# Last feature pair of two token groups: from tile products to seven block products

## The chip, the cores and the metric

The kernel runs on one core of a Trainium2 chip. The time is the device time of one launch, in microseconds. The engines are named as in the profile: PE (TensorE, the matrix products), PEld (its weight loads), DVE (VectorE), ACT (ScalarE), POOL (GpSimd) and SP (SyncE, whose queue issues the transfers). PE writes its products into PSUM, of which a core has eight banks here, each 128 x 512 fp32. POOL works on SBUF alone.

## The reference, cut to what matters

Retention over 4 x 8 heads gives 3072 tokens of 512 features. Two feed-forward layers follow:

```
h = x @ w_in;   g = h * sigmoid(1.702 h);        x = g @ w_out          (d_ff 2048)
gate = sigmoid(x @ w_gate);  val = x @ w_val;    out = (gate*val) @ w_out   (d_ff 1536)
```

All is fp32. The change lies in the second layer, the last part of the kernel.

## The kernel before, in words

**Splits.** A product of fp32 matrices is made of three matmuls on operands split in two, high part times high, high times low, low times high. A split of a tile is two instructions: ACT casts the tile to its high part (h), and another engine subtracts that from the tile to get the low part (l).

**The second layer.** The tokens go in NG = 3 groups g of 1024, the 1536 features in QS = 6 pairs q of 256. For each group and pair there are two chains n, one for the gate (m = 0) and one for the value (m = 1), 36 chains in all. A chain multiplies the group's x by a 512 x 256 slice of the weights as a 2 x 2 block product with seven block products instead of eight (Winograd's form). `product` (L652) is one of them: six matmuls of 128 x 512. The seven are named by their operands: A11 B11 in `begin` (L728); A12 B21, S2 T2, S1 T1 and S3 T3 in `middle` (L737); A22 T4 and S4 B22 in `finish` (L768). A11 B11, S2 T2, S3 T3 and A22 T4 add up in one PSUM bank `a`; S1 T1 and S4 B22 in another, `d`. Between the additions ACT copies bank `a` out, once after each of A11 B11 (m1), S2 T2 (u2) and S3 T3 (u3), and `c22` (L763) is added by DVE from bank `d` and u3. `consume` (L700) takes each of the four results: for a gate chain the sigmoid, for a value chain the product of gate and value (DVE, L712) and its split (ACT L721, DVE L723).

**The group's x operands.** T1 = B12 - B11, T2 = B22 - T1, T3 = B12 - B22 and T4 = B21 - T2 are made from x by POOL, and B11, B21, T1, T2, T3, T4 and B22 are split in two halves k. The tiles of the splits exist once, so an operand of the next group can only be split once the last chain of the present one has used it. `prep_late` (L546) is a generator that makes them for groups 1 and 2: first the loads from `x2d`, then the differences, then the splits. The border loop calls it step by step.

**The output product.** The features of a pair times 256 rows of w_out are again a block product with seven parts, `out_seven` (L845), for the pairs q = 0 to 4: seven steps, each of two times six matmuls of 128 x 256 (L853), and after each step DVE adds the two banks to `part` in SBUF (L868; once per pair, by an ACT copy L865 and a POOL addition L866 instead). It needs four sums of the feature blocks, S1 to S4, made by POOL in `g_sums` (L680) and split in `g_parts` (L691), one at each call of `pump` (L667), and eight products of w_out blocks, made ahead by `out_job` (L793) during the last units of the first layer and kept in DRAM as `wtd`. `load_wt` (L839) brings them in, one copy at a time. For pair q = 5 no such sums are made: `out_pair` (L903) multiplies the eight 128-token tiles of the group by both features directly, six matmuls of 128 x 512 for each tile (L911), and `evict` (L918) adds the bank to `part` on DVE and stores the tile's rows.

**The order around the border of two groups** is written out by hand in the loop from L1171: each engine runs its instructions in the order in which the loop emits them. For the pair q = 5, with chains n and n + 1: `middle(n)`, the seven steps of pair 4 around `finish(n)`, `begin(n+1)`, `load_wt(5)`, the loads of the next chain's weights, `middle(n+1)`, two half tile products, `finish(n+1)`, the rest of the tile products with an eviction and a step of `prep_late` behind each, and `begin(n+2)`. The borders are those behind chains 11 and 23; the third group has none.

## Time and profile before

| | us |
|---|---|
| median of 3 runs (1145.3 to 1145.57) | 1145.51 |
| the profiled execution | 1146.02 |
| its span, first to last instruction | 1144.3 |
| PE busy | 1138.4 |
| DVE busy | 803.3 |
| ACT busy | 584.8 |
| POOL busy | 582.9 |

The span is what the engines' instructions cover; the profiled execution's time holds 1.7 us more around it. Busy times are sums over instructions; PE's instructions overlap in the pipeline, so its busy time is not work at its peak rate. An instruction's row gives its start, its time, its line in the kernel and, in brackets, how long its engine had idled before it and what ended that. A row of several instructions gives their sum. The chain that ended last is followed backwards from the end: it shows which engine's work the time consists of.

### The profile page before, as it was taken

How to read it: one execution, taken by the hardware profiler on the slowest of the kernel's cores; microseconds unless marked ns; L12 is line 12 of the kernel's file. 1: busy time of each engine (PE TensorE's matmuls, PEld its weight loads, DVE VectorE, ACT ScalarE, POOL GpSimd, SP SyncE). 2: the span in 40 equal slices, each digit the busy share in tenths (PEclk: the TensorE clock that was granted, in tenths of full speed). 3: DMA queues.
4: the chain of work that ended last, by engine and by line, in shares of the span. 5: the costliest groups of instructions: out<-in, count | busy, mean ns of one | idle time of the engine just before them, and what ended most of it. 6: DMA issues, size and time to landing. Idle time of an engine off the chain costs nothing.

```text
span 1144.3 us, 17967 instructions
## 1 busy us (share of the span) xinstructions
PE 1138.4 (99%) x6610; PEld 964.2 (84%) x6610; DVE 803.3 (70%) x1085; ACT 584.8 (51%) x1048; POOL 582.9 (51%) x439
## 2 busy tenths in 40 slices
PE   9999999999999999999999999999999999999998
PEld 8778888888888888888888888888888888888887
DVE  6988768777777667775663788776566676566666
ACT  4676665566565556655554544445433334543331
POOL 5578765555645445554454687776222256222220
PEclk9999999999999999999999999999999999999999
DMA  9855745565454544523205476678655556655533
GB/s 343 270 162 180 228 127 186 173 212 194 150 192 147 166 146 160 194 82 120 83 19 191 173 281 226 224 262 309 224 191 193 193 203 247 249 193 194 193 129 111
DMA packets 83139, 215.09 MB, mean 188 GB/s; under 512 B 9194, under 2 KB 13802, under 8 KB 83052
## 3 DMA queue, kind: packets, MB, share of 16 engines
q1 hardware_dynamic: 82608, 213.55, 54.7%
q8 instruction: 52, 0.85, 0.3%
q10 hardware_dynamic: 444, 0.40, 0.1%
q14 instruction: 35, 0.29, 0.1%
HBM read 155.46 MB, written 58.46 MB: 187 GB/s over the span
## 4 chain that ended last, share of the span: by engine, by line
PE 92%; DVE 3%; POOL 2%; issue 1%; DMA 1%; ACT 1%; SPq 0%; DVEq 0%; POOLq 0%; ACTq 0%
PE pa L658 16%; PE pd L658 8%; PE po L853 8%; PE acc L435 7%; PE h L325 7%; PE h L327 7%; PE h L326 7%; PE acc L437 7%; PE acc L436 7%; PE pb L658 4%; PE pa L853 2%; PE pd L853 2%; PE h L133 2%; PE po L911 2%; PE h L191 1%
## 5 line engine op out<-in xcount | busy, mean ns | idle before, releaser
L310 POOL TENSOR_TENSOR wl<-wraw,wh 128x512 fp32r<-128x512 f32 x110 | 156.6, 1431 | 176.6 <-ACT wh L309 167.0
L683 POOL TENSOR_TENSOR raw<-raw,raw 128x512 f32<-128x512 f32 x60 | 89.9, 1519 | 180.0 <-DVE raw L712 178.8
L325 PE MATMUL h<-xh,wh 128*128 128x512 f32 x380 | 149.0, 392 | 0.0
L435 PE MATMUL acc<-gh,wh 128*128 128x512 f32 x376 | 148.4, 395 | 0.2 <-DVE half L450 0.2
L327 PE MATMUL h<-xh,wl 128*128 128x512 f32 x380 | 148.1, 390 | 0.2 <-POOL wl L310 0.2
L326 PE MATMUL h<-xl,wh 128*128 128x512 f32 x380 | 147.9, 389 | 0.0
L437 PE MATMUL acc<-gl,wh 128*128 128x512 f32 x376 | 146.5, 390 | 0.0
L436 PE MATMUL acc<-gh,wl 128*128 128x512 f32 x376 | 146.3, 389 | 0.0
L344 DVE TENSOR_TENSOR gl<-sg,gh 128x512 fp32r<-128x512 f32 x94 | 102.5, 1091 | 52.8 <-ACT gh L343 51.6
L336 DVE TENSOR_TENSOR sg<-h,sg 128x512 f32<-128x512 f32 x94 | 64.8, 689 | 85.8 <-ACT sg L335 85.7
L309 ACT CAST wh<-wraw 128x512 fp32r<-128x512 f32 x190 | 110.8, 616 | 14.5 <-PE acc L437 11.0
L335 ACT ACTIVATE sg<-h 128x512 f32<-128x512 f32 x94 | 56.2, 598 | 113.9 <-PE h L327 111.2
L658 PE MATMUL pa<-xoh,oh 128*128 128x512 f32 x288 | 112.5, 391 | 0.0
L658 PE MATMUL pa<-xol,oh 128*128 128x512 f32 x288 | 112.4, 390 | 0.0
L658 PE MATMUL pa<-xoh,ol 128*128 128x512 f32 x288 | 112.1, 389 | 0.0
L343 ACT CAST gh<-sg 128x512 fp32r<-128x512 f32 x94 | 58.2, 621 | 74.8 <-DVE sg L336 74.7
L327 PEld LDWEIGHTS h<-xh,wl 128*128 128x128 f32 x380 | 71.3, 188 | 16.1 <-POOL wl L310 1.2
L435 PEld LDWEIGHTS acc<-gh,wh 128*128 128x128 f32 x376 | 70.6, 188 | 16.8 <-ACT wh L309 0.6
L325 PEld LDWEIGHTS h<-xh,wh 128*128 128x128 f32 x380 | 71.3, 188 | 15.3 <-issue 0.5
L326 PEld LDWEIGHTS h<-xl,wh 128*128 128x128 f32 x380 | 71.3, 188 | 15.2 <-issue 0.5
L437 PEld LDWEIGHTS acc<-gl,wh 128*128 128x128 f32 x376 | 70.6, 188 | 15.1
L436 PEld LDWEIGHTS acc<-gh,wl 128*128 128x128 f32 x376 | 70.6, 188 | 14.2
(217 smaller groups left out, 2835.4 us busy)
## 6 DMA issues: line engine op xcount, KB each, us to landing
w<-in_w_dram SPq DMA_DIRECT2D x68, 512.0 KB, 4.1
in_t<-in_qkv_dram SPq DMA_DIRECT2D x95, 256.0 KB, 4.4
oh<-wcd SPq DMA_DIRECT2D x24, 512.0 KB, 3.8
ol<-wcd SPq DMA_DIRECT2D x24, 512.0 KB, 4.8
w2d<-cva SPq DMA_DIRECT2D x36, 256.0 KB, 2.2
oh<-wcd SPq DMA_DIRECT2D x24, 384.0 KB, 3.2
ol<-wcd SPq DMA_DIRECT2D x24, 384.0 KB, 4.0
raw<-w2d SPq DMA_DIRECT2D x26, 256.0 KB, 3.5
```

What stands on the lines that cost most here:

```text
L309: nc.scalar.copy(wh, raw)
L310: lo_engine.tensor_tensor(out=wl, in0=raw, in1=wh, op=ALU.subtract)
L325: nc.tensor.matmul(bank[:, :n], wh[:, k, :], xh[:, k, :n], start=(k == 0), stop=False)
L326: nc.tensor.matmul(bank[:, :n], wh[:, k, :], xl[:, k, :n], start=False, stop=False)
L327: nc.tensor.matmul(bank[:, :n], wl[:, k, :], xh[:, k, :n], start=False, stop=(k == KC - 1))
L344: nc.vector.tensor_tensor(out=gl[:, :n], in0=sg[:, :n], in1=gh[:, :n], op=ALU.subtract)
L435: nc.tensor.matmul(a, wh[:, wc], gh[:, :n], start=st, stop=False)
L436: nc.tensor.matmul(a, wl[:, wc], gh[:, :n], start=False, stop=False)
L437: nc.tensor.matmul(a, wh[:, wc], gl[:, :n], start=False, stop=sp)
L658: nc.tensor.matmul(bank, w[:, kk], x[:, k, :], start=start and k == 0 and w is wh and x is xh, stop=stop and k == 1 and w is wl, skip_grou ...
L683: nc.gpsimd.tensor_tensor(out=out_, in0=in0, in1=in1, op=op)
L853: nc.tensor.matmul(bank[:, t * 256:(t + 1) * 256], a[:, sl], b[:, w, :], start=start and not t and a is gh and b is wh, stop=a is gl, skip ...
```

## The change

For q = 5 of groups 0 and 1 the tile products are replaced by `out_seven` with its seven steps, its `part` sums and now its stores (`store`), with bank `b` used again in place of a new `d`. Therefore `consume` makes the sums S1 to S4 there too, `out_job(5)` prepares all eight blocks (two groups of units more, `OUT_AT`), and `load_wt` brings seven of them. The steps are laid around the first chain of the next group: step 1 behind `finish(n+1)`, step 2 behind `begin(n+2)`, and steps 3 to 7 inside `middle(n+2)`, between S2 T2 and S1 T1 (`ahead2`). `prep_late` splits each operand in one step, half k = 0 on DVE and half k = 1 on POOL; its loads for k = 1 go into the free `raw8` tile. B11 and B21 are split inside `middle(n+1)` ahead of S1 T1, T2 behind it, and T1, T3, T4 and B22 between steps 3 to 7. The third group keeps the tile products, which read their four blocks from other places of `wtd`.

```diff
         0: (34, 35, 38, 39, 40, 42), 1: (41, 42, 43, 46, 47, 48), 2: (51, 52, 54, 55, 56, 58),
-        3: (66, 67, 68, 70, 71, 72), 4: (72, 73, 74, 75, 76, 78), 5: (82, 83, 84),
+        3: (66, 67, 68, 70, 71, 72), 4: (72, 73, 74, 75, 76, 78), 5: (82, 83, 84, 85, 86, 87),
     }
...
     NC0 = 2 * QS
-    OT1, OT2, OT3, OT4, OB21, OB22, OB11 = range(7)
+    OT1, OT2, OT3, OT4, OB21, OB22, OB11, OB12 = range(8)
     wcd = [dram.tile([P, 14, 256], F32, name=f"wcd{n}") for n in range(NC0)]
-    wtd = [[dram.tile([P, 7, 256], F32, name=f"wtd{q}{x}") for x in "hl"] for q in range(QS)]
+    wtd = [[dram.tile([P, 8 if q == QS - 1 else 7, 256], F32, name=f"wtd{q}{x}") for x in "hl"] for q in range(QS)]
     p2 = {}
...
         p2["w"].append(pool(ctx, "wo", 1, "left"))
-        p2["xu"] = pool(ctx, "xu", 3, "left")
+        p2["xu"] = pool(ctx, "xu", 2, "left")
         for name, bufs in (("part", 1), ("tmp", 1), ("g7", 1), ("wt", 1), ("raw7", 5), ("ct", 2)):
...
+        t = p2["w"][0].tile([P, 8, 256], F32, name="raw8", tag="raw8")
         for k in range(2):
-            for j, half, kk in ((B11, 0, k), (B12, 1, k), (B22, 1, k + 2), (B21, 0, k + 2)):
-                raws[k][j] = tile1("raw7" if k and j == B21 else "xu" if k else "xt")
+            for e, (j, half, kk) in enumerate(((B11, 0, k), (B12, 1, k), (B22, 1, k + 2), (B21, 0, k + 2))):
+                raws[k][j] = t[:, 2 * e:2 * e + 2, :].rearrange("p a c -> p (a c)") if k else tile1("xt")
                 nc.sync.dma_start(out=raws[k][j], in_=x2d[2 * g + half][:, kk, :])
...
-        def split(k, j, engine):
-            h, l = hl[j]
-            nc.scalar.copy(h[:, k, :], raws[k][j])
-            engine.tensor_tensor(out=l[:, k, :], in0=raws[k][j], in1=h[:, k, :], op=ALU.subtract)
+        def split(j, engine=nc.gpsimd):
+            for k in range(2):
+                h, l = hl[j]
+                nc.scalar.copy(h[:, k, :], raws[k][j])
+                (engine if k else nc.vector).tensor_tensor(
+                    out=l[:, k, :], in0=raws[k][j], in1=h[:, k, :], op=ALU.subtract
+                )
...
             for j in (T1, T2):
-                raw[j] = p2["ct"].tile([P, 512], F32, name="ct", tag="ct") if k else tile1("xt")
+                raw[j] = tile1("xu" if k else "xt")
             diff(k, T1, B12, B11)
...
             yield
-        for j in (B11, B21):
-            for k in range(2):
-                split(k, j, nc.gpsimd)
-            yield
-            yield
-        for k in range(2):
-            split(k, T2, nc.gpsimd if k else nc.vector)
+        split(B11)
+        yield
+        split(B21)
+        yield
+        split(T2)
         for k in range(2):
...
         for j in (T1, T3, T4, B22):
-            for k in range(2):
-                split(k, j, nc.gpsimd if k else nc.vector)
-                yield
+            split(j)
+            yield
...
         yield
-        if j == A21 and q < QS - 1:
+        if j == A21 and chains[n] != (NG - 1, QS - 1, 1):
             g_sums()
...
-    def middle(n):
+    def middle(n, ahead2=lambda: None, behind2=lambda: None):
...
         pump()
+        ahead2()
         product(n, d, S1, T1, True, True)
...
         pump()
+        behind2()
         cb[n] = [a, d, u2, c22]
-    def finish(n, last):
+    def finish(n, last, border=False):
         a, d, u2, c22 = cb.pop(n)
...
         add(d, d, u2)
-        pump()
+        if not border:
+            pump()
         next(x12)
...
         next(x12)
-        if last:
+        if last or border:
             next(x12)
...
             t = p2["w"][0].tile([P, 8, 256], F32, name="raw8", tag="raw8")
-            w0, w1_ = t[:, :2], t[:, 2:4]
+            w0, w1_, sa, sb = (t[:, 2 * j:2 * j + 2] for j in range(4))
         else:
...
+        yield
         if plain:
-            h = p2["w"][0].tile([P, 4, 256], F32R, name="oh0", tag="oh0")[:, :2]
-            todo = [(w0, slice(0, 2), slice(0, 2)), (w1_, slice(0, 2), slice(2, 4))]
+            t = p2["w"][0].tile([P, 4, 256], F32R, name="oh0", tag="oh0")
+            hs = [t[:, :2], t[:, 2:4]]
         else:
-            yield
             sa = in_p.tile([P, 2, 256], F32, name="half", tag="half", bufs=3)
             sb, h = (g_p.tile([P, 2, 256], x, name="ost", tag="ost") for x in (F32, F32R))
-            op(sa[:, 0], w0[:, 1], w0[:, 0])
-            op(sa[:, 1], w1_[:, 1], sa[:, 0])
-            yield
-            todo = [
-                (w0, slice(0, 1), slice(OB11, OB11 + 1)),
-                (w1_, slice(0, 2), slice(OB21, OB22 + 1)),
-                (sa, slice(0, 2), slice(OT1, OT2 + 1)),
-                (sb, slice(0, 2), slice(OT3, OT4 + 1)),
-            ]
+            hs = [h, h]
+        op(sa[:, 0], w0[:, 1], w0[:, 0])
+        op(sa[:, 1], w1_[:, 1], sa[:, 0])
+        yield
+        n = 2 if plain else 1
+        todo = [
+            (w0, slice(0, n), slice(OB11, OB11 + n)),
+            (w1_, slice(0, 2), slice(OB21, OB22 + 1)),
+            (sa, slice(0, 2), slice(OT1, OT2 + 1)),
+            (sb, slice(0, 2), slice(OT3, OT4 + 1)),
+        ]
         for j, (t, sl, to) in enumerate(todo):
+            h = hs[j % 2]
             nc.scalar.copy(h[:, sl], t[:, sl])
...
             l = t.bitcast(F32R)
-            if not plain and not j:
+            if not j:
                 op(sb[:, 0], w0[:, 1], w1_[:, 1])
...
-    def load_wt(q):
+    def load_wt(q, plain=False):
         wt[:] = [p2["wt"].tile([P, 7, 256], F32R, name=f"wt{x}", tag=f"wt{x}") for x in "hl"]
-        n = 4 if q == QS - 1 else 7
+        pieces = [(0, OB11, 2), (2, OB21, 2)] if plain else [(0, 0, 7)]
         for x in range(2):
-            nc.sync.dma_start(out=wt[x].bitcast(F32)[:, :n, :], in_=wtd[q][x][:, :n, :])
-
-    def out_seven(q):
+            for to, a, n in pieces:
+                nc.sync.dma_start(out=wt[x].bitcast(F32)[:, to:to + n, :], in_=wtd[q][x][:, a:a + n, :])
+
+    def out_seven(q, g=None):
...
+        def store(s, half, e):
+            if g is not None:
+                r0 = g * 1024 + half * 512 + s * 256
+                nc.sync.dma_start(
+                    out=out[r0:r0 + 256, e * 256:(e + 1) * 256].rearrange("(t p) c -> p t c", t=2),
+                    in_=part[half, s][:, :, e * 256:(e + 1) * 256],
+                )
+
         a = [bank2("po") for _ in range(2)]
...
         yield
-        b = [bank2("po"), bank2("pb")]
+        b = [bank2("po"), bank2("pb" if g is None else "pd")]
         for s in range(2):
...
             gather(s, 0, 0, b[s])
+            store(s, 0, 0)
+        if g is not None:
+            yield
         for s in range(2):
...
             gather(s, 0, 1, a[s], True, True)
-        d = [bank2("pd"), bank2("pa")]
+        if g is not None:
+            yield
+        d = [bank2("pd"), bank2("pa")] if g is None else b
         for s in range(2):
...
             gather(s, 1, 1, d[s], True)
+        if g is not None:
+            yield
         for s in range(2):
...
             gather(s, 1, 1, a[s])
+            store(s, 1, 1)
+        if g is not None:
+            yield
         for s in range(2):
...
             gather(s, 0, 1, d[s])
+            store(s, 0, 1)
+        if g is not None:
+            yield
         for s in range(2):
...
             gather(s, 1, 0, a[s], True)
+            store(s, 1, 0)
         yield
...
         sums(1)
+        crossed = []
         for n, (g, q, m) in enumerate(chains):
...
             load_chain(n + 2)
-            middle(n)
+            middle(n, *crossed)
+            crossed = []
             keep(n)
...
                     next(xs)
-                    steps.append(xs)
             if not border:
...
             if n:
-                load_wt(q)
+                load_wt(q, q == QS - 1 and not border)
             if border:
                 fetch(n + 2)
+                middle(n + 1, lambda: (next(xs), next(xs)), lambda: next(xs))
+                keep(n + 1)
+                finish(n + 1, False, True)
+                fetch(n + 3)
+                seven = out_seven(q, g)
+                next(seven)
+                begin(n + 2)
+                pump()
+                next(seven)
+                pump()
+
+                def across(seven=seven, xs=xs):
+                    pump()
+                    pump()
+                    for _ in range(4):
+                        next(seven)
+                        next(xs)
+                    next(seven)
+
+                crossed = [across]
+                continue
             middle(n + 1)
...
             fetch(n + 3)
-            steps.clear()
-            if border:
-                next(xs)
             for tt, kind in ((2, "po"), (3, "pb")):
...
                 evict(g, tt, ob[tt])
-                if border and tt < TOK - 1:
-                    next(xs)
-            if border:
-                steps.append(xs)
-            begin(n + 2)
```

## Rows read from the trace of the kernel before

**Rows 1.** The page: span, its first section, the granted TensorE clock in 40 slices.
```profile
span 1144.3 us, 17967 instructions
PE 1138.4 (99%) x6610; PEld 964.2 (84%) x6610; DVE 803.3 (70%) x1085; ACT 584.8 (51%) x1048; POOL 582.9 (51%) x439
...
PEclk9999999999999999999999999999999999999999
```

**Rows 2.** Chain of waits across the second border: start us, us, what.
```profile
943.37 1.44 PE po L853 x12
944.81 1.39 PE pa L658 x6
...
950.28 1.36 PE pa L658 x6
951.64 1.36 PE po L911 x6
```

**Rows 3.** PE's timeline in the first border, around its one pause.
```profile
780.98 0.39 PE L911 MATMUL po<-wtl,g7h 128*128 128x512 f32 x1
781.52 0.50 PE L911 MATMUL po<-wth,g7l 128*128 128x512 f32 x1
781.86 0.40 PE L911 MATMUL po<-wth,g7h 128*128 128x512 f32 x1
```

**Rows 4.** PE's timeline, first and second border: the matmul behind S3 T3.
```profile
775.32 0.39 PE L911 MATMUL po<-wth,g7h 128*128 128x512 f32 x1
...
951.48 0.39 PE L911 MATMUL po<-wth,g7h 128*128 128x512 f32 x1
```

**Rows 5.** ACT's timeline in the second border: casts of B11, then u3.
```profile
950.01 0.62 ACT L569 CAST xoh<-xt 128x512 fp32r<-128x512 f32 x1
950.53 0.62 ACT L569 CAST xoh<-xu 128x512 fp32r<-128x512 f32 x1
951.73 0.59 ACT L761 COPY u<-pa 128x512 f32<-128x512 f32 x1 [0.57 <-PE pa L658]
```

**Rows 6.** ACT's timeline in the first border: u3 and the last cast of B21.
```profile
775.76 0.58 ACT L761 COPY u<-pa 128x512 f32<-128x512 f32 x1
...
776.76 0.62 ACT L569 CAST xoh<-raw 128x512 fp32r<-128x512 f32 x1
```

**Rows 7.** Groups of one shape in the second layer, 569 to 1120 us.
```profile
L868 DVE TENSOR_TENSOR part<-po,part 128x512 f32<-128x512 f32 x92 | 61.6, 684 | 6.4 <-ACT part L862 5.2
L678 DVE TENSOR_TENSOR g7l<-raw,g7h 128x512 fp32r<-128x512 f32 x60 | 60.6, 1023 | 26.3 <-ACT g7h L677 25.7
...
L683 POOL TENSOR_TENSOR raw<-raw,raw 128x512 f32<-128x512 f32 x60 | 89.9, 1519 | 180.0 <-DVE raw L712 178.8
...
L677 ACT CAST g7h<-raw 128x512 fp32r<-128x512 f32 x60 | 36.2, 620 | 5.4 <-POOL raw L683 5.4
...
L706 ACT ACTIVATE sg<-pb 128x512 f32<-128x512 f32 x18 | 10.9, 603 | 3.0 <-DVE pb L698 3.0
```

**Rows 8.** First border: a DVE instruction with two SBUF inputs beside one of POOL.
```profile
777.10 1.41 DVE L712 TENSOR_TENSOR raw<-c,sg 128x512 f32<-128x512 f32 x1
...
776.66 1.30 POOL L570 TENSOR_TENSOR xol<-xu,xoh 128x512 fp32r<-128x512 f32 x1
```

**Rows 9.** Last units of layer one: busy times in 500 to 560; first sum of chain 0.
```profile
500.00:560.00 60.00, 60.00 (x290) 49.38 (x289) 37.37 (x51) 34.71 (x63) 27.54 (x20) 1.00 0.37 116
...
578.92 0.73 POOL L612 TENSOR_TENSOR raw<-raw 128x256 f32<-128x256 f32 x1
```

**Rows 10.** POOL's timeline: chain 10's last split, first difference of half k = 1.
```profile
749.17 1.85 POOL L650 TENSOR_TENSOR ol<-raw,oh 128x768 fp32r<-128x768 f32 x1 [5.51 <-ACT oh L649]
...
770.87 1.29 POOL L565 TENSOR_TENSOR ct<-xu 128x512 f32<-128x512 f32 x1
```

**Rows 11.** Output weights: issue of pair 5's load, landing of pair 4's (735 to 768 us).
```profile
769.05 0.43 SPq L843 DMA_DIRECT2D wtl<-wtd5l  x1
...
wtl<-wtd4l SPq DMA_DIRECT2D x1, 896.0 KB, 8.1
```

## The prediction, made before the changed kernel was run

> **What bounds the kernel now.** I read the page first. PE is busy 1138.4 of 1144.3 us, its granted clock is 9 in every slice, and the next engine, DVE, stands at 70% [rows 1]. So time goes only with PE's work or with pauses forced on PE. Next the chain that ended last, through the second layer: PE products follow each other there without gaps. A block product is 1.36 us, a step of `out_seven` 1.44, a block product right behind such a step 1.39 [rows 2]. The two half tiles ahead of `finish` are six matmuls in 1.36, so 0.227 us for one of 512 columns. Third, PE's timeline at the two borders which the change rebuilds. There is one pause: a matmul begins 0.54 us behind the one before it and the next 0.34, where 0.23 is usual, 0.4 us in all [rows 3]. The matmul that had to wait is the third of its group, the first that reads a low part; the two ahead of it ran. Fourth, ACT, DVE and POOL at the borders, since every operand that the new steps read is made there.
>
> The profiled execution took 1146.02 us for its span of 1144.3; the median of the three runs is 0.5 us lower. My sum is a difference, and I put it on the median.
>
> **The change, part by part.**
>
> *PE's work.* Out go 48 matmuls of 512 columns for each border, 48 x 0.227 = 10.9 us; in come seven steps, 7 x 1.44 = 10.1 [rows 2]. That is 0.8 saved, 1.6 for two borders. Three block products now stand behind a step where one did (0.03 each): 0.2 back on rounding up. The pause of 0.4 [rows 3] goes with the tile products. So PE has 1.8 us less, and nothing else in the change can make the kernel faster.
>
> *A wait for u3.* S3 T3 and A22 T4 add into one bank, and ACT must have copied u3 out between them. Before, two half tiles stood between (1.36 us); the change takes them away and puts nothing there. PE is free for A22 T4 at 775.32 and at 951.48 [rows 4]. In the second border u3 ran 951.73 to 952.32 behind two casts [rows 5], so even a prompt copy costs 0.85. But B21's two casts now stand ahead of it as well. Casts follow each other every 0.52 us [rows 5], so u3 starts at 950.01 + 4 x 0.52 = 952.09, ends at 952.68, and PE waits **1.25** with 0.05 for the signal. In the first border u3 takes the place of the last of the four casts [rows 6]: 776.76 + 0.59, a wait of **2.05**.
>
> *DVE up to step 2.* Step 2 needs A12's low part. In the second border DVE starts on B11 when its cast is done, 950.01 + 0.62 = 950.63. From there it runs, in the emitted order, the subtractions of B11, B21 and A11, c22, the subtraction of T2, the products of A22 and A12, A22's subtraction, the addition to `d`, the product of A21, A12's subtraction: eleven, of which seven have both inputs in SBUF. The three for B11, B21 and T2 are new on DVE. One with a PSUM input takes 0.68. One with two SBUF inputs beside POOL is the unknown: the 60 splits of `g_parts` average 1.02 [rows 7]; alone I take it as no dearer than the gather, 0.68; and beside POOL it took 1.41 once, since it began while a POOL instruction of 1.30 ran and ended 0.55 behind that one [rows 8]. I take 1.02, the mean of most instructions and of the same kind of work: 7 x 1.02 + 4 x 0.68 = 9.9, ready at 960.5. Its first two matmuls don't read the low part (0.24), so PE can start at 960.3. PE arrives at 951.48 + 1.25 + 2 x 1.36 + 1.44 + 1.39 = 958.3. The wait, part of it already at S4 B22 for c22, is **2.0**. The first border gives the same within 0.1, since DVE and PE both start from u3's neighbourhood there.
>
> For that unknown the low end is 7 x 0.68 + 2.7 = 7.5: no wait. For the high end POOL has five instructions in this stretch (three splits, two differences), so five of the seven can be held: 5 x (1.30 + 0.55) + 6 x 0.68 = 13.3, a wait of 5.4. The Trainium skill (SBUF — State Buffer, Who interferes with whom) says that such a DVE instruction and a POOL instruction that reads SBUF lock each other out for their whole length. The trace agrees [rows 8]. Were each of the five to meet a fresh lock, it would be the high end; the mean of 1.02 says that many meet a lock's remainder or none.
>
> *S2.* Step 3 needs the split of S2, a second sum behind A21's product: that is ready at 959.5, two POOL sums of 1.52 and a cast of 0.62 [rows 7] give 963.2. DVE has, behind A12, step 1's two gathers, S3's split and step 2's two gathers: 960.5 + 1.4 + 1.0 + 1.4 = 964.3, then S2's subtraction to 965.3, or 965.1 for PE. PE is there at 960.3 + 1.44 + 2 x 1.36 = 964.5: **0.6**. Ends: 0 and 1.3, the latter with 1.41 for both subtractions.
>
> *S1.* ACT casts S1 only behind u2 and the sigmoid of the next group's first chain, and that sigmoid waits for an addition that stands behind S2's subtraction on DVE. So behind S2: 0.68 + 0.60 + 0.62 + 0.68 = 2.6, against step 3's 1.44 [rows 7]: **1.2**. Without a late S2 it is u2 (0.25 + 0.59) instead of the addition: 1.1. There is no cheaper end.
>
> *Banks.* Step 7 adds into banks that step 5's gathers must have read, and T1's and T3's subtractions stand between those gathers on DVE. From S1 (967.9): S4 0.7, T1 1.0, two gathers, T3 1.0, one gather: 972.7. PE would be there at 967.7 + 3 x 1.44 = 972.0: **0.8**. Ends 0.3 (all at 0.68) and 0.9.
>
> *What I put at nothing.* `out_job(5)` gets four POOL subtractions, two casts, two DVE subtractions and their DMAs more in layer one, where in 500 to 560 us DVE is busy 37, ACT 35 and POOL 28 of 60 [rows 9]. `load_chain(0)` queues behind its last store, some three units later, and its first reader, 578.92 [rows 9], stays behind. The loads for k = 1 wait for POOL's split of chain 10 to end at 751.0, 20 us ahead of their first difference [rows 10]. `load_wt(5)` grows to 896 KB for each of two: landing 8.1 us behind 769.05 [rows 11] is 777.2, ahead of step 1 at about 780; without that cover step 1 would wait for what is late. The stores queue on SP ahead of fetches that wait for PE anyway, needed a pair later.
>
> *Sum.* Second border 1.25 + 2.0 + 0.6 + 1.2 + 0.8 = 5.85; first 6.65. Together 12.5, less 1.8 of PE's: **+10.7 us, 1145.5 to 1156.2**. With every low end: 2.65 and 3.45, +4.3, 1149.8. With the high ends: DVE's wait 5.4, S2 at most 0.6 since POOL catches up meanwhile, banks 0.9, so 9.35 and 10.15, +17.7, 1163.
>
> **The rivals.**
>
> *Not slower: DVE, ACT and POOL keep up.* The mechanism is PE as the only bound. It decides at A12's low part and at u3: if DVE's eleven instructions take under 7.5 us and u3 is copied promptly, and S1 hides, only twice 0.9 for u3 remains against 1.8 saved: 1145.5. With nothing left at all it is 1143.7, 0.16% below, and that is the floor. For it speaks that the same seven steps pause nowhere in the other pairs, DVE being at 70%. Against it: there DVE has no splits for the next group beside them, and the order u3 behind four casts is fixed.
>
> *Slower by more: the SBUF lock at each instruction.* POOL gets nine splits and differences, four sums and two additions almost in a row, and DVE fifteen instructions with two SBUF inputs between middle(n+1) and step 7. If they alternate, 1163. There is such a meeting [rows 8]; the mean of 1.02 speaks against it as the rule.
>
> *Transfers.* Were step 1 held for the weights at the first border, each us late would be one lost, some 3 us in all, 1159. The landing of 8.1 leaves room.
>
> That the new steps don't replace the tiles cannot be: the emitted order is fixed.
>
> **How the numbers follow.** Waits by the middle values, 1150 to 1160: 0.6. The lock at each instruction, 1160 to 1163: 0.2. Transfers: 0.05. The keeping up at 1145.5: 0.12. More than 0.2% gained: 0.03, since the floor is 1143.7 and 0.2%, about what a measurement of this kernel can tell from no change, is 2.3 us. So slower 0.85, same 0.12, faster 0.03. The range 1148 to 1162 leaves out the two last and the end of the lock case; its low end lies under 1149.8 because the S1 and u3 waits are my own reading of an order that no row shows.
>
> **What would show it.** In the profile after: PE idle before A22 T4 of chains 11 and 23 released by ACT's u copy, 1.2 to 2; PE idle before the second step released by DVE's low part; before the third and fourth by `g_parts`' low parts; PE's total work 1.6 us less. DVE's splits at the border averaging about 1.0. I am wrong if PE has no idle rows at L658 and L853 there, or if they add up to under 4 us; and if time is lost in the first layer's units, the extended `out_job` was not free.

## The result, and the profile after

The changed kernel takes 1159.1 us (median of 4 runs, 1158.7 to 1161.3) against 1145.5 on the same chip: a ratio of 1.0121, 95% interval 1.0109 to 1.0134. It is slower by 13.6 us where 10.7 were forecast. The profiled execution took 1161.27 us; its span is 15.0 longer than that of [rows 1]. The page, its first section, POOL's busy tenths and the granted clock in 40 slices:

```profile
span 1159.3 us, 18179 instructions
## 1 busy us (share of the span) xinstructions
PE 1144.8 (99%) x6682; PEld 970.4 (84%) x6682; DVE 829.5 (72%) x1105; ACT 590.3 (51%) x1060; POOL 602.9 (52%) x451
...
POOL 5677765555546445545464677796222257222220
PEclk9999999999999999999999999999999999999999
```

PE's busy time rose by 6.4 us although it has less to do: a busy PE is not a PE at its peak. Layer one is as it was. PE is at the place of [rows 4] of the first border at 775.08, 0.24 us sooner than before, and the window of [rows 9] shows POOL with 2.8 us more and PE without a pause:

```profile
500.00:560.00 60.00, 60.00 (x290) 49.36 (x289) 37.95 (x51) 35.04 (x65) 30.35 (x24) 1.00 0.27 92
```

So everything was lost at the borders. PE's waits there, all of them (columns: engine, line, what it waited for: us in total, times, longest; L659 is the block product, L861 the seven steps, L763 u3's copy, L699 the addition into c22, L724 the subtraction behind A11, A12 and A22, L876 a gather, L678 and L679 the splits of the sums):

```profile
PE pa L659 <- ACT u L763: 3.0, 2, 1.9
PE pd L659 <- DVE c L699: 2.0, 2, 1.0
PE po L861 <- DVE g7l L724: 1.7, 1, 1.7
PE po L861 <- DVE part L876: 1.3, 1, 1.3
PE po L861 <- ACT g7h L678: 0.6, 2, 0.3
PE po L861 <- DVE g7l L679: 0.4, 2, 0.2
```

These are 9.0 us of 17.1 lost. The others show in PE's timeline by the distance from one start to the next, usually 0.23 us for 512 columns and 0.12 for 256. The second border, around its first three pauses:

```profile
957.67 0.39 PE L659 MATMUL pa<-xoh,ol 128*128 128x512 f32 x1
959.15 0.50 PE L659 MATMUL pa<-xoh,oh 128*128 128x512 f32 x1 [1.09 <-ACT u L763]
959.49 0.40 PE L659 MATMUL pa<-xol,oh 128*128 128x512 f32 x1
...
960.42 0.39 PE L659 MATMUL pa<-xoh,ol 128*128 128x512 f32 x1
961.84 0.50 PE L659 MATMUL pd<-xoh,oh 128*128 128x512 f32 x1 [1.03 <-DVE c L699]
...
966.26 0.28 PE L861 MATMUL po<-wtl,g7h 128*128 128x256 f32 x1
968.26 0.39 PE L861 MATMUL po<-wth,g7l 128*128 128x256 f32 x1 [1.72 <-DVE g7l L724]
```

From 957.67 to 959.15 are 1.48 us, 1.25 too many, of which the bracket calls 1.09 idle. The matmul behind it also comes late: 959.15 to 959.49 is 0.34, so each restart costs 0.1 more. And for some microseconds in each border every matmul took nearly twice its time. First come two rows of the first border, then two stretches (columns: the stretch, its length in us, the busy times of PE, PEld, DVE, ACT and POOL, the granted clock, the DMA share, GB/s):

```profile
780.46 0.63 PE L659 MATMUL pd<-xol,oh 128*128 128x512 f32 x1
780.89 0.63 PE L659 MATMUL pd<-xoh,ol 128*128 128x512 f32 x1
```

```profile
780.00:786.00 6.00, 6.00 (x22) 5.29 (x23) 5.88 (x7) 1.22 (x2) 4.04 (x4) 0.55 1.04 408
...
969.00:974.00 5.00, 5.00 (x20) 4.06 (x19) 4.36 (x5) 1.24 (x2) 4.58 (x4) 0.66 0.25 83
```

Starts 0.43 us apart are the 1.2 GHz level; the granted clock was 0.50 from 778.6 to 785.4 and from 969.8 to 973.2, which the two stretches shown mix with full clock. Added up start to start, with the restart in each entry:

| lost, us | first border | second border |
|---|---|---|
| u3 | 2.2 | 1.4 |
| c22 (DVE's queue) | 1.2 | 1.3 |
| A12's low part (DVE's queue) | hidden by the 1.2 GHz stretch | 2.0 |
| stretch at 1.2 GHz | 2.6 | 1.6 |
| S2 | 0.1 | 0.2 |
| S1 | 1.1 | 1.0 |
| banks and gathers | 0.6 | 1.8 |
| sum | 7.8 | 9.3 |

Span less lost time is 1159.3 - 17.4 = 1141.9 (0.3 are lost elsewhere), before 1144.3 - 0.7 = 1143.6. So PE's work, with all lost time taken out, fell by 1.7, about what the prediction gave.

Where DVE's time went, second border, DVE and then POOL:

```profile
957.09 0.69 DVE L572 TENSOR_TENSOR xol<-xt,xoh 128x512 fp32r<-128x512 f32 x1 [1.58 <-ACT xoh L571]
958.13 1.35 DVE L572 TENSOR_TENSOR xol<-xt,xoh 128x512 fp32r<-128x512 f32 x1 [0.34 <-ACT xoh L571]
959.40 1.78 DVE L724 TENSOR_TENSOR g7l<-raw,g7h 128x512 fp32r<-128x512 f32 x1
961.10 0.68 DVE L699 TENSOR_TENSOR c<-pd,u 128x512 f32<-128x512 f32 x1
961.71 1.16 DVE L572 TENSOR_TENSOR xol<-xt,xoh 128x512 fp32r<-128x512 f32 x1
962.79 1.78 DVE L713 TENSOR_TENSOR raw<-c,sg 128x512 f32<-128x512 f32 x1
...
967.53 0.68 DVE L724 TENSOR_TENSOR g7l<-raw,g7h 128x512 fp32r<-128x512 f32 x1
```

```profile
957.65 2.98 POOL L572 TENSOR_TENSOR xol<-raw,xoh 128x512 fp32r<-128x512 f32 x2 [5.45 <-ACT xoh L571]
960.60 1.72 POOL L572 TENSOR_TENSOR xol<-xu,xoh 128x512 fp32r<-128x512 f32 x1
```

The first begins ahead of POOL's instructions and takes 0.69. The next four with two SBUF inputs begin while POOL is at work and are stretched to 1.16 to 1.78; c22, with a PSUM input, keeps its 0.68. The last is A12's low part, for which PE waits. This is [rows 8] once more, at nearly every turn.

### The profile page after: what moved, and what is told of

The parts are those of the page before. It is cut to its first block, busy times and chain, and to the rows that moved or that the text cites. A ratio compares the mean times of both kernels' runs of the same rounds, so it can differ in the third digit from the quotient of the medians.

```text
span 1159.3 us, 18179 instructions
## 1 busy us (share of the span) xinstructions
PE 1144.8 (99%) x6682; PEld 970.4 (84%) x6682; DVE 829.5 (72%) x1105; ACT 590.3 (51%) x1060; POOL 602.9 (52%) x451
## 4 chain that ended last, share of the span: by engine, by line
PE 89%; DVE 3%; DMA 3%; POOL 2%; issue 1%; ACT 1%; SPq 0%; DVEq 0%; ACTq 0%; POOLq 0%
PE pa L659 15%; PE po L861 9%; PE pd L659 8%; PE acc L435 7%; PE h L325 7%; PE h L326 7%; PE h L327 7%; PE acc L437 7%; PE acc L436 7%; PE pb L659 4%; PE pd L861 2%; PE pa L861 2%; PE h L133 2%; DMA in_t<-in_qkv_dram 1%; PE h L191 1%
## 5 line engine op out<-in xcount | busy, mean ns | idle before, releaser
L684 POOL TENSOR_TENSOR raw<-raw,raw 128x512 f32<-128x512 f32 x68 | 102.2, 1524 | 184.8 <-DVE raw L713 183.5
L659 PE MATMUL pa<-xoh,oh 128*128 128x512 f32 x288 | 113.2, 393 | 3.0 <-ACT u L763 3.0
L659 PE MATMUL pa<-xol,oh 128*128 128x512 f32 x288 | 112.7, 391 | 0.0
L659 PE MATMUL pa<-xoh,ol 128*128 128x512 f32 x288 | 112.3, 390 | 0.0
L861 PE MATMUL po<-wth,g7l 128*128 128x256 f32 x314 | 89.9, 286 | 2.2 <-DVE g7l L724 1.7
L861 PE MATMUL po<-wth,g7h 128*128 128x256 f32 x314 | 89.9, 286 | 2.0 <-DVE part L876 1.3
L679 DVE TENSOR_TENSOR g7l<-raw,g7h 128x512 fp32r<-128x512 f32 x68 | 68.0, 1014 | 30.0 <-ACT g7h L678 29.3
L861 PE MATMUL po<-wtl,g7h 128*128 128x256 f32 x314 | 89.3, 284 | 0.0
```

The costliest lines, as they stand in the source:

```text
L659: nc.tensor.matmul(bank, w[:, kk], x[:, k, :], start=start and k == 0 and w is wh and x is xh, stop=stop and k == 1 and w is wl, skip_grou ...
L684: nc.gpsimd.tensor_tensor(out=out_, in0=in0, in1=in1, op=op)
L861: nc.tensor.matmul(bank[:, t * 256:(t + 1) * 256], a[:, sl], b[:, w, :], start=start and not t and a is gh and b is wh, stop=a is gl, skip ...
```

## Experiments

**Part by part, from the changed kernel.** First, u3 ahead of the casts.

```diff
-                middle(n + 1, lambda: (next(xs), next(xs)), lambda: next(xs))
+                middle(n + 1, lambda: None, lambda: (next(xs), next(xs), next(xs)))
```

> The splits of B11 and B21 move behind u3 and c22, nothing else. Theory (one DVE queue up to A12's low part decides, the waits ahead of it are only where PE happens to meet it): PE's wait for u3 falls to about 0.85 us per border and the wait for c22 goes, but the wait for A12's low part grows by as much: 1159 us, within 1 of the changed kernel. Rival (each wait is a cost of its own): the two u3 waits lose 1.1 and 0.3, the two c22 waits 1.0 each: 3.4 us less, 1155.5.

1161.7 us, ratio 1.0138 (1.0123 to 1.0153), 2.6 above the changed kernel where at most 1 was expected. PE's waits:

```profile
PE po L861 <- DVE g7l L724: 3.7, 2, 1.9
PE po L861 <- ACT g7h L722: 3.7, 2, 1.8
PE pa L659 <- ACT u L763: 1.5, 2, 0.7
```

u3's waits halve and c22's go, but what stands behind on ACT and DVE is late by as much: A11 at step 1 and A12 at step 2 now wait nearly 2 us each, in both borders. Taking one wait out of the queue moves it on.

Second, step 1 of the seven put between S3 T3 and A22 T4.

```diff
+                seven = out_seven(q, g)
+                next(seven)
                 finish(n + 1, False, True)
                 fetch(n + 3)
-                seven = out_seven(q, g)
-                next(seven)
```

> Step 1 of the seven stands between S3 T3 and A22 T4, so that 1.44 us of PE work lie where u3 is copied. Theory (the DVE queue decides): what is hidden there is missing ahead of step 2, so 1159 us within 1. Rival (u3's order is a cost of its own): 1.95 and 1.09 us of waiting go, 1156.

1161.2 us, ratio 1.0132 (1.0117 to 1.0147). The wait for u3 is gone, since PE has 1.44 us of other work, and what is hidden there is missing ahead of step 1, not only of step 2: step 1 waits for A11's low part, up to 3.4 us:

```profile
PE po L861 <- DVE g7l L724: 7.0, 4, 3.4
PE po L861 <- DVE g7l L679: 1.3, 4, 0.4
```

The eight runs of these two kernels all had a mean granted clock under 1 (0.994 to 0.999), so stretches at 1.2 GHz may be what lifts both above their expected 1159; that is argued, not tested. Neither came near its rival's 1155.5 or 1156.

Third, POOL's part of the next group's splits without its reads: a memset stands in place of the subtraction, so these low parts are left out.

```diff
-                (engine if k else nc.vector).tensor_tensor(
-                    out=l[:, k, :], in0=raws[k][j], in1=h[:, k, :], op=ALU.subtract
-                )
+                if k:
+                    nc.gpsimd.memset(l[:, k, :].bitcast(F32), 0.0)
+                    continue
+                nc.vector.tensor_tensor(out=l[:, k, :], in0=raws[k][j], in1=h[:, k, :], op=ALU.subtract)
```

> POOL's subtractions for half k = 1 of the next group's seven operands become a memset of the low part: left out are these low parts of groups 1 and 2. The DVE instructions stay as they are. Theory (DVE's queue is long because its instructions with two SBUF inputs wait for POOL's): the subtractions at the border fall from 0.9 to 1.3 us towards 0.7, PE's waits for c22 and A12's low part go, those for u3, S2, S1 and the banks stay: about 8 us less, 1151. Rival (the count of DVE instructions alone is too high, POOL does not matter): 1158 to 1159.

1154.9 us, ratio 1.0082 (1.0066 to 1.0099): 4.2 us less than the changed kernel, with PE's and DVE's instructions unchanged, about half of the 8 that were expected. c22's wait is gone and A12's is 1.0 us, in the second border; in the first, a 1.2 GHz stretch (granted 0.50 from 777.8 to 781.0) stands ahead of it. u3's waits stayed, as expected. The groups of DVE in the second border of this kernel:

```profile
L725 DVE TENSOR_TENSOR g7l<-raw,g7h 128x512 fp32r<-128x512 f32 x3 | 2.1, 685 | 0.1
L714 DVE TENSOR_TENSOR raw<-c,sg 128x512 f32<-128x512 f32 x1 | 1.8, 1772 | 0.0
```

The three subtractions of A11, A12 and A22 took 1160 ns on average in the changed kernel and 685 here. The product for A22, which still meets a POOL difference that reads, keeps 1.77. So POOL's reads beside DVE, and not the number of DVE's instructions, make most of that queue's delay; what is left (u3, S1, banks) they don't make. The Trainium skill (SBUF — State Buffer, Who interferes with whom) says that POOL contends when it reads SBUF and not when it only writes; this run agrees: subtractions beside a memset took 0.69 us at 774.79 and 0.68 at 974.55.

Fourth, the part in layer one by itself: the kernel before with all eight weight blocks of pair 5 made there (four before) and the four that it uses loaded from their new places.

```diff
+        op(sa[:, 0], w0[:, 1], w0[:, 0])
+        op(sa[:, 1], w1_[:, 1], sa[:, 0])
+        yield
+        n = 2 if plain else 1
+        todo = [
+            (w0, slice(0, n), slice(OB11, OB11 + n)),
...
+        pieces = [(0, OB11, 2), (2, OB21, 2)] if plain else [(0, 0, 7)]
```

> The kernel before with one part of the change alone: out_job for pair 5 prepares all eight blocks in layer one and the tile products read their four from the new places. Theory (layer one has room): 1145.5 us within 0.5. Rival (the longer job or the later load of chain 0 costs): a PE pause ahead of 620 us and 1146.5 or more.

1145.87 us, ratio 1.0003 (0.9994 to 1.0012). It costs nothing that can be told from the spread of the runs.

Fifth, without the feature sums.

```diff
-            g_sums()
-            steps.append(g_parts())
+            if q < QS - 1:
+                g_sums()
+                steps.append(g_parts())
```

> The changed kernel with the four feature sums of pair 5 and their splits left out: S1 to S4 of pair 5 are not formed, and steps 3 to 6 of the seven multiply pair 4's S1 to S4 instead. It takes from POOL four sums, from ACT four casts and from DVE four subtractions at each border; PE's work stays. My theory (each wait is set by the queue of DVE, ACT or POOL ahead of it): the waits for u3, c22 and A12's low part stay, being ahead of the sums, and the waits for S1 and for the banks go, with POOL's share in A12's wait. These were about 2.0 at the second border and 1.3 at the first, with up to 1 more at each from restarts and POOL; so 3.5 to 5 us less than the 1159.1 of the changed kernel: 1154 to 1155.5. Rival (the sums ride along hidden, the waits around them belong to the splits of the next group's operands): 1158 to 1159.5. Rival (all waits hang on POOL's sums): under 1149.

1156.85 us, ratio 1.0096 (1.0080 to 1.0111): 2.3 us less than the changed kernel, between the two first expectations. The waits at S1 went, as expected. The one for the banks didn't: step 7 still waited 1.3 us for a gather, now in the first border and no longer in the second. The sums shift that wait and don't make it. What does is seen on DVE in the second border of the changed kernel, where the gather for which PE waited stands behind a split of 1.85 us:

```profile
980.11 1.85 DVE L572 TENSOR_TENSOR xol<-xt,xoh 128x512 fp32r<-128x512 f32 x1
981.88 1.27 DVE L876 TENSOR_TENSOR part<-po,part 128x512 f32<-128x512 f32 x2
```

Without the sums such a split stands in the first border, ahead of the gather for which PE waits there:

```profile
795.54 1.83 DVE L572 TENSOR_TENSOR xol<-xt,xoh 128x512 fp32r<-128x512 f32 x1
```

**The same work in another order.** If only order loses, an order should win it back. This kernel takes the borders of the changed one apart: DVE does both halves of the next group's splits, each short of its reader; POOL keeps differences and sums; the chain after is begun between S3 T3 and A22 T4; the steps are spread through the next group's first chain. PE's order and u3's copy, the lines between them left out, where n is the pair's last chain and n+1 the next group's first:

```diff
+        product(n, b, A12, B21, True, True)
+        product(n, a, S2, T2, False, True)
+        product(n, d, S1, T1, True, True)
+        product(n, a, S3, T3, False, True)
+        nc.scalar.copy(u3, a)
+        begin(n + 1)
+        product(n, a, A22, T4, False, True)
+        product(n, d, S4, B22, False, True)
+        product(n + 1, b2, A12, B21, True, True)
+        product(n + 1, a2, S2, T2, False, True)
+        seven(1)
+        product(n + 1, d2, S1, T1, True, True)
+        product(n + 1, a2, S3, T3, False, True)
+        seven(2)
+        begin(n + 2)
+        seven(4)
+        seven(3)
+        product(n + 1, a2, A22, T4, False, True)
+        seven(5)
+        product(n + 1, d2, S4, B22, False, True)
+        seven(6)
+        seven(7)
```

> The same seven steps and the same arithmetic as in the changed kernel, in another order at each border: both halves' splits of the next group's operands go to DVE, each right ahead of its first reader; POOL keeps differences and sums alone; u3 is copied with no cast queued ahead of it; the next group's first chain is begun between S3 T3 and A22 T4; and the seven steps lie spread through that chain (1, 2, 4, 3, 5, 6, 7), so that nothing is read soon after it is made. My theory (the change loses only by its order, the work of PE is 1.8 us less): laid out by hand with the durations of the trace, about 1.5 us of waits are left at each border, so 1143.7 + 3 = about 1147, 1145 to 1150, and no wait over 1 us. Rival (seven products instead of tile products at a border cost by themselves, since DVE, ACT and POOL haven't the time for the next group's splits beside them whatever the order): 1155 or more, with waits of DVE's low parts in other places. Between 1150 and 1155 the order is most of it and the layout missed something.

1152.9 us, ratio 1.0066 (1.0053 to 1.0079): between the two expectations, so my layout missed something; order has given back 6 of the 13.6 us so far. PE's waits:

```profile
PE pa L653 <- DVE c L693: 1.8, 1, 1.8
PE pa L653 <- DMA oh<-wcd: 1.6, 1, 1.6
PE pa L653 <- DMA ol<-wcd: 1.3, 2, 0.8
PE po L938 <- DVE g7l L673: 0.4, 2, 0.2
```

All but the last stand at the chain begun early. Its weights were issued on SP behind pair 5's output weights and landed 6.8 us or more behind their issue:

```profile
768.53 0.43 SPq L845 DMA_DIRECT2D wtl<-wtd5l  x1
769.06 0.38 SPq L638 DMA_DIRECT2D oh<-wcd  x1
```

A stretch at 1.2 GHz followed here too, in each border (granted 0.50 from 778.6 to 781.4 and from 959 to 962). So the load was moved.

```diff
+            if border:
+                fetch(n + 2)
             if n:
                 load_wt(q, q == QS - 1 and not border)
             if border:
-                fetch(n + 2)
```

> The spread order with one thing moved: at a border the load of the next chain's weights is issued ahead of the load of pair 5's output weights, not behind it. In the spread order the chain begun early waited on PE for these weights, which landed some 7 us behind their issue with 1.75 MB ahead of them; behind that wait a stretch of the profile ran at half clock. My theory (the transfer is what that wait is for, and the half clock follows the pause): of 10.7 us lost at the borders some 8 go, 1152.9 less 6 to 8.5: 1144.5 to 1147, with about 0.8 left at each border at S1's step. Rival (it waits for DVE's c22 and for B11's splits, as the second border's wait is labelled): one border gains at most, 1148.5 to 1153. Rival (the output weights, now later, are waited for at step 1): a new wait there, 1148 or more.

1146.6 us, ratio 1.0009 (1.0000 to 1.0018): one move in SP's queue gave 6.3 us, the stretches at 1.2 GHz included, which are gone as well. The wait of the second border that the profile put down to DVE's c22 was this transfer as well: it went with it. Left were

```profile
PE pd L653 <- DVE c L693: 0.8, 1, 0.8
PE po L938 <- DVE g7l L673: 0.4, 2, 0.2
```

the first at S4 B22, where DVE's queue reaches c22 late in the first border, the second at S1's step. Next, step 3 went ahead of step 4, with S2's and S1's splits earlier.

```diff
-        sig(3, c22)
+        part_g(S2, S2)
         seven(2)
         part_g(S1, A21)
-        part_g(S2, S2)
+        sig(3, c22)
...
+        seven(3)
...
         seven(4)
...
-        seven(3)
```

> As the kernel with the weights' load moved, and step 3 of the seven (S2) ahead of step 4 (S1), the casts of S2 and S1 ahead of the sigmoid of c22, and step 2's gathers behind S2's subtraction. It aims at the 0.8 us lost at each border where step 4 found S1's split and its banks not ready. My theory (every wait of the change was a matter of order): nothing over 0.3 us is left at a border, PE's work is 1.8 us less than before, so 1143.7 to 1145.5, about 1144.5, that is 0.05 to 0.15% under the kernel before. Rival (something is always late at a border, since the new splits are added work): 0.5 to 1 us at each border in a new place, 1145 to 1147.

1146.95 us, ratio 1.0013 (1.0004 to 1.0022). S1's waits are gone, and PE waits for B22's split in their place, 0.7 us in each border: the rival. So that one, and c22, were moved up as well.

```diff
-        split(B21)
         d = bank2("pd")
...
         add(c22, d, u3)
+        split(B21)
...
+        gl(A22)
         seven(3)
         part_g(S3, A11)
+        split(B22)
         seven(4)
         part_g(S4, A12)
-        split(B22)
-        gl(A22)
```

> As the kernel before this one, with the waits that its profile shows taken out of the queues of DVE and ACT: B21 is split behind c22 and not ahead of it, B22 is split ahead of S4 and of step 4's gathers, and A22's subtraction goes into a gap of DVE. In that profile 3.2 us are lost at the borders: 1.1 at the first border where S4 B22 waits for c22, 1.0 at each where S4 B22 of the next chain waits for B22's split. My theory (only order): 1146.6 to 1146.9 less 3: 1143.7 to 1144.8, which is 0.06 to 0.15% under the kernel before, the 1.8 us of PE's work at last in the time. Rival (each order only moves the lost time on, since DVE has no slack at a border): 1145.5 to 1147, with waits of 0.5 to 1 us in new places.

1149.0 us, ratio 1.0030 (1.0018 to 1.0042), 2 us worse. The second border, DVE and then POOL:

```profile
968.97 1.78 DVE L992 TENSOR_TENSOR g7l<-raw,g7h 128x512 fp32r<-128x512 f32 x1
970.67 1.75 DVE L673 TENSOR_TENSOR g7l<-raw,g7h 128x512 fp32r<-128x512 f32 x1
```

```profile
968.78 3.10 POOL L949 TENSOR_TENSOR part<-ct,part 128x512 f32<-128x512 f32 x2 [1.58 <-ACT ct L948]
```

The subtractions had come to lie beside POOL's two additions for step 3, and each took 1.75 us or more where 0.68 is usual; PE waited 1.5 for the second. With these additions on DVE, and A22's subtraction behind S4's:

```diff
-                gather(s, half, e, banks[s], i == 3)
+                gather(s, half, e, banks[s])
...
-        gl(A22)
         seven(3)
...
         part_g(S4, A12)
+        gl(A22)
```

> As the kernel before this one, but step 3's two gathers stay on DVE instead of a copy by ACT and an addition by POOL, and A22's subtraction goes behind S4's. In the kernel before this one POOL's two additions for step 3 ran beside the subtractions of A22, S3 and B22, and these took 1.7 to 1.8 us in place of 0.68; 6.0 us were lost there. My theory (DVE is held by POOL's instructions that read SBUF, and with none of them left behind the sums the queue just fits): the 1.7 us subtractions go, up to 0.7 us is lost at each border, 1143.7 to 1145.2. Rival (two gathers more on DVE, 1.2 us, make it late without any lock): 1146 to 1149, subtractions at 0.68 and waits for S3's or S4's low part all the same.

1147.7 us, ratio 1.0020 (1.0011 to 1.0029). DVE's part came out as my theory had it: no wait for a low part is left, though DVE has two gathers more. The time didn't, because of a wait that was 0.6 us in one border of the kernel before it and has grown:

```profile
PE po L855 <- DMA wtl<-wtd0l: 1.5, 2, 1.3
```

This is the next pair's output weights, issued behind four stores whose gathers now come later. Issued ahead of them:

```diff
-                for s in range(2):
-                    store(s, half, e)
+                stores.extend((s, half, e) for s in range(2))
+            if i < 6:
+                flush()
...
+        load_wt(0)
+        flush()
```

> As the kernel before this one, but the load of the next group's first output weights is issued ahead of the last four stores of the seven steps and not behind them. In the profile of the kernel before this one no wait of PE for DVE, ACT or POOL is left at the borders; what is left is 1.9 us of waits for that load, which stood in SP's queue behind the stores, and some 1.6 us of late starts of 0.1 to 0.3 each. My theory (now the stores' place in the queue sets it): 1147.7 less 1.9: 1145.3 to 1146.3. Rival (the load is slow for other reasons, its transfer beside the stores): 1147 to 1148.

1145.86 us against 1145.74 of the kernel before in the same runs, ratio 1.0002 (0.9993 to 1.0011). No wait of PE is listed behind 700 us. What is lost at the borders is 1.2 and 0.8 us, in late starts of 0.1 to 0.3. The last trial, c22 of the next chain behind T4's and S3's splits, was to remove these:

```diff
-        add(c22, d2, u3)
         part_g(S2, S2)
...
         part_g(S3, A11)
+        add(c22, d2, u3)
         split(B22)
         seven(4)
         part_g(S4, A12)
+        sig(3, c22)
         gl(A22)
```

> As the kernel before this one, and in the next group's first chain c22 is added behind T4's and S3's splits, not ahead of S2's, which gives S2, S1 and T4 0.6 us more. It aims at the late starts of 0.1 to 0.3 us, 1.2 us in the first border and 0.35 in the second. My theory: 0.5 to 1.2 us less than the kernel before this one, 1144.3 to 1145.5, at most 0.1% under the kernel before the change. Rival (one of these subtractions now meets a sum on POOL and takes 1.7 us): 1146 to 1148, with a wait of about 1 us at S2's or S1's low part.

1146.5 us, ratio 1.0009 (1.0000 to 1.0018): the rival in time and kind, with other sizes. S2's subtraction took 1.12 and 1.09 us beside POOL's sums, and not 1.7, and PE waited not for it but for S4's low part, behind it on DVE, 0.5 in each border. No order tried here beats the kernel before.

## Why the prediction was right, and where its sizes were off

The forecast held: slower, in the range, by the named mechanism (operands late at the borders, PE's work 1.6 less). That the sum of waits came near, 12.5 forecast against 17.1 - 4.2 = 12.9 without the 1.2 GHz stretches, is in part luck: terms that were too small (DVE's queue, the banks) and too large (S2, A12's wait of the first border) made up for each other.

- **PE's work.** 1.7 us less by spans, close to the 1.6 of the steps. The floor of 1143.7 was never reached; the best order stands 2 us above it.
- **u3.** 2.05 and 1.25 forecast, 2.1 and 1.25 measured without the restart. The order of ACT's casts was read rightly. In the second border u3 follows the last cast, and PE starts 0.05 us behind it, at 959.15:

```profile
958.00 0.62 ACT L571 CAST xoh<-raw 128x512 fp32r<-128x512 f32 x1
958.52 0.58 ACT L763 COPY u<-pa 128x512 f32<-128x512 f32 x1
```

- **DVE's queue.** The step that was mis-sized: 2.0 forecast, 1.2 + 1.9 = 3.1 measured in the second border. The eleven instructions took 967.53 + 0.68 - 957.09 = 11.1 us and not 9.9. The seven with two SBUF inputs averaged 1.21 and not 1.02: 0.69, 1.35, 1.78, 1.16, 1.78, 1.02 and 0.68. The mean of [rows 7] mixes two cases. In the trace of before, 18 of its 60 splits met no POOL instruction and took 0.68; the 42 that met one averaged 1.17. In the borders, whose slices of the page show POOL busy 5 to 9 tenths, nearly all meet one: 7 x 1.17 + 4 x 0.68 = 10.9 would have been close. The lock case of the rivals was half right. The kernel without POOL's reads, 4.2 us faster, confirms that those reads are the cause. That part of the wait comes already at c22 was right. In the first border DVE took the same 11.1 (775.13 to 786.19), but only c22's 1.2 shows, since the stretch at 1.2 GHz held PE up meanwhile.
- **S2**: 0.6 forecast, at most 0.2 measured. A12's later low part delays PE, and in the second border so does the stretch at 1.2 GHz, so these rows don't test the term by itself; in the second border of the kernel without POOL's reads, with the clock at 1.00 and a shorter wait for A12, S2 cost 0.6 and a restart. **S1** was right (1.2 forecast, 1.0 to 1.1 with restarts). The **banks** were 0.8 forecast, 0.6 and 1.8 measured; that they hang on the splits ahead of the gathers was right, by the rows above; that a split there can take 1.85 was not in it.
- **At nothing.** Layer one's extra work costs nothing by its own run. No transfer was waited for in the changed kernel; that rival fell.
- **What had no term.** The restart of 0.1 behind each pause, and the stretches at 1.2 GHz, 4.2 us in the profiled execution. They go with the profiled one's lying 2.1 above the median: the two runs with the full mean clock took 1158.7 and 1158.8, 2.5 less than the profiled one. So some 2.5 of the 4.2 are a loss, an estimate from these runs; the rest covers other waits, A12's in the first border above all.

## What to carry to other kernels

Where an engine is bound to 99%, a rewrite that saves it 0.15% of work has to place every operand of the new steps ahead of its use: draw the queues of the other engines through the stretch, SP's included, before counting the saving. Price a two-input DVE instruction by what POOL does in that very stretch (0.68 alone, up to 1.85 in these borders beside a POOL instruction that reads), not by its mean over the layer. When a wait is taken out and the time stays, look at what stands next in the same queue: here the first reordering and the move of one load won back all but 1 us. Four more moves, of which two made it worse or no better, won back the rest, and nothing beyond the kernel before.

## What the hardware showed that was not expected

- **Pauses of PE can cost more than their length.** In the changed kernel the granted clock fell to 0.50, the 1.2 GHz level, at 778.6, 1.4 us after a pause of 2.1 had ended and just ahead of one of 1.2, and at 969.8 behind pauses of 1.25, 1.2 and 1.9, with PE back at work. In the first spread order it fell behind 1.8 and 0.9 and behind 1.9 and 0.7. In the kernel without POOL's reads a single pause of 2.1 came ahead of it (granted 0.50 from 777.8 on):

```profile
776.86 0.50 PE L660 MATMUL pa<-xoh,oh 128*128 128x512 f32 x1 [1.95 <-ACT u L764]
...
778.00 0.63 PE L660 MATMUL pa<-xol,oh 128*128 128x512 f32 x1
778.43 0.63 PE L660 MATMUL pa<-xoh,ol 128*128 128x512 f32 x1
```

A single one of 1.7 in the kernel with B21's and B22's splits moved left it at 1.00. So did pauses of 1.25, 1.2 and 1.9 in the second border of the kernel without the feature sums, the same three behind which it fell in the changed kernel. The Trainium skill (TensorE: Matmul & The Clock Gate, Part 1: The HAM clock gate) says that the clock follows how busy PE has lately been; the rows agree in kind, but the lengths of the pauses alone do not tell when it falls.

- **A restart costs 0.1 us** behind a pause: the second start comes 0.34 after the first and not 0.23.
- **Where a two-input DVE instruction meets a reading one of POOL, the later of the two is the long one.** In the kernel with step 3 ahead of step 4, S2's subtraction began at 964.42, 0.05 us ahead of POOL's third sum; it took 0.68, and the sum 1.79. In the last kernel it began 0.7 us behind a sum and took 1.09 and 1.12. Counted over the changed kernel from 609 us on (128 x 512 on both engines), 43 of the 54 such DVE instructions that began behind a POOL one still at work took over 0.8 us, and none of the 20 that began ahead of one did. With starts 0.02 us apart or less it went either way: a DVE split of 0.68 beside a POOL split of 1.84 at 796.97, one of 1.85 beside 1.31 at 980.11.
